# Moving part of GpSimd's elementwise work to VectorE in a fused attention and feed-forward kernel, with a new instruction order

## The chip, the cores and the metric

One NeuronCore of one Trainium2 chip runs the whole program. The metric is device time in microseconds (us) of one execution, as the median of several. TensorE does the matrix products, VectorE and ScalarE the elementwise work, GpSimd some more of it, and SyncE only issues the transfers (DMAs) between memory and the core's on-chip memory. Each engine works through its own list of instructions in order, and semaphores make one engine wait for another.

## What is computed

The reference is attention followed by a normalised feed-forward layer, in float32:

```python
def _attn_ref(q, k, v):                  # (4, 8, 768, 64)
    block, window = 32, 16
    k_sum = k.reshape(B, H, nb, block, D).max(axis=3)
    v_sum = v.reshape(B, H, nb, block, D).mean(axis=3)
    scores_l = where(|i - j| < window, scale * q @ k.T, -1e9)
    scores_s = scale * q @ k_sum.T + log(block)
    a = softmax(concat([scores_l, scores_s]))
    return a @ concat([v, v_sum])

def _moe_ref(x, g_ln, w_ch1, w_ch2):     # x: (4, 768, 512)
    xn = (x - mean(x)) / sqrt(var(x) + 1e-06) * g_ln
    return x + maximum(xn @ w_ch1, 0.0) @ w_ch2
```

Each row sees a window of 31 keys around it and 24 block summaries, and the result of the 8 heads is one row of 512 values, which is normalised, multiplied by a 512 x 2048 and a 2048 x 512 matrix, and added to itself.

## The kernel before, in words

The 3,072 rows are 24 tiles T of 128 rows (`TT`), six to a batch; two tiles are a group g (`NG` = 12) for the feed-forward part. To get the exactness of float32 from 16-bit products, an operand is split into a high part in float16 and a low part, which is what the high part leaves over, and three products of high and low parts are added.

**Stages.** The first batch (T = 0 to 5) is attended in float32 (`attend`, L932), while the weights come in, are merged from their 64-bit form, scaled and split (`fetch_w` to `split_w`, L648 to L755). From T = 6 on, attention goes by split parts (`attend_late`, L942): `load_q`, `load_k`, `load_v` split the inputs; `heads` (L455) makes the scores on TensorE; `late_softmax` (L503) takes the maximum on VectorE, the exponential on ScalarE, the high part of the probabilities on ScalarE and their low part on GpSimd (L521), and sends both through a transposing DMA; `values` (L469) multiplies them with v two tiles later (`LAG`), and `late_out` (L610) divides by the row sums. So the softmax of tile T stands in the list with `values` and `norm` of tile T - 2.

`ln` (L622) normalises a tile: VectorE takes mean and variance; GpSimd adds the constant 1e-6 (L628) and raises to the power -1/2 (L629); VectorE subtracts the mean; ScalarE makes the high part and VectorE the low part of the result (`x16`, L634). `lnT` (L638) sends it through a transposing DMA into `xt`, from which TensorE makes the first product of the feed-forward part (`g1`, L758; tile `h` in the trace). `norm` is the two of them.

For groups 0 to 2 the second product is plain (`g2`). From group 3 on (`PLAIN`) `parts_of` (L785) and `g2_wide` (L827) use a scheme with seven products in place of eight, summed in four PSUM tiles (`acc_a`, `acc_s`, `acc_o`; five for the last group). When the last step of a group (j = 7) is done, the sums are added to the rows: u on ScalarE, v and w on VectorE, and the two additions of u, v and w to the tiles' rows x0 and x1 on GpSimd (L869, L873); the rest on VectorE, and two DMAs store the tiles.

`batch_s` (L371) makes the scales of a batch: VectorE sums, TensorE adds over the partitions (tile `vps`), and VectorE works on that (tile `vm`, L378 and after).

**The order.** The functions only record instructions in a list (`Plan.record`). `Plan.issue` (L158) then issues them in the order of `ORDER`, a packed list of indices worked out beforehand. It sets the place of each instruction on its engine and of each DMA on SyncE; semaphores follow from who reads and writes what. A run of matmuls recorded in a `unit` is one entry. `SOFT` and `WIDE` are 0 before, so that the conditions in L521, L869 and L873 send all of this work to GpSimd.

Every instruction is issued in L163, so the trace tells them apart by their tiles: `p<-p,p` is the low part of the probabilities, `x<-x,uv` the addition to the rows, `rs<-mv` the constant of the normalisation.

Of the kernel before, what the change touches and what calls it, by code (L numbers as in the profile page):

```python
# [24 lines left out]
P = 128  # L25
# [29 lines left out]
SOFT, WIDE = 0, 0  # L55
# [111 lines left out]
def body(ctx: ExitStack, tc, qt, qa, qe, kt, ks, va, vb, vs, g_ln, w1, w2, blocks, out):  # L167
# [335 lines left out]
    def late_softmax(t):  # L503
# [17 lines left out]
        (nc.vector if T < SOFT else nc.gpsimd).tensor_tensor(lo, p, hi, ALU.subtract)  # L521
# [99 lines left out]
    @pl.step  # L621
    def ln(T):  # L622
        x = xt[T]
        s6 = work("s6", f"s6_{T}", [P, 6], F32, 2)
        mv = work("mv", f"mv{T}", [P, 2], F32, 2)
        rs = work("rs", f"rs{T}", [P, 1], F32, 2)
        nc.vector.bn_stats(s6[:], x[:])
        nc.vector.bn_aggr(mv[:], s6[:])  # L628
        nc.gpsimd.tensor_scalar(rs[:], mv[:, 1:2], 1e-6, 0.0, ALU.add, ALU.add)  # L629
        nc.gpsimd.tensor_tensor(rs[:], rs[:], mhalf[:], ALU.pow)  # L630
        xn = stg("xn", [P, DM])
        nc.vector.scalar_tensor_tensor(xn[:], x[:], mv[:, 0:1], gb[:], ALU.subtract, ALU.mult)
# [469 lines left out]
```

## Time and profile before

| | |
|---|---|
| median of 3 runs | 592.65 us (590.61 to 593.58) |
| the profiled execution | 591.7 us, its span 589.9 us |
| TensorE (PE) busy | 577.5 us, 98% |
| VectorE (DVE) busy | 505.0 us, 86% |
| ScalarE (ACT) busy | 437.2 us, 74% |
| GpSimd (POOL) busy | 134.6 us, 23% |
| granted TensorE clock | 1.00 of full speed |

The span runs from the first to the last instruction that the profiler saw; the execution's own time has 1.8 us more around it. Times in the rows are us from the start of the span; a duration is the profiler's, and instructions of one engine overlap a little, so that the start of the next one is often earlier than the end of the last. "PEld" is TensorE's loading of weights, beside its products. "[0.36 <-DVE vm L163]" behind a row means that the engine was idle for 0.36 us before it, and that this wait was ended by VectorE's write of tile vm.

### The profile page before, as it was taken

To read this page: it belongs to the slowest core of one execution; us is meant where nothing else is said; L and a number is where in the kernel's file an instruction comes from. 1 tells how busy PE (TensorE), PEld (TensorE's weight loads), DVE (VectorE), ACT (ScalarE), POOL (GpSimd) and SP (SyncE) were. 2 spreads that over 40 slices of the span, in tenths; PEclk is the share of its full clock that TensorE was granted. 3 is DMA by queue.
4 is the path that set the end of the run, shared out by engine and by line. 5 is a ranking of instruction groups with operands and counts; after the bars stand their busy time and mean duration, and the time that the engine had idled before them with its cause. 6 is when DMAs were issued, how large, how long until landed. Compare 5 with 4: busy or idle time off the path is not lost.

```text
span 589.9 us, 16263 instructions
## 1 busy us (share of the span) xinstructions
PE 577.5 (98%) x6152; PEld 467.0 (79%) x6152; DVE 505.0 (86%) x1326; ACT 437.2 (74%) x1079; POOL 134.6 (23%) x225
## 2 busy tenths in 40 slices
PE   7989999999999999999999999999999999999997
PEld 5557768875555688888889888888788888888886
DVE  4899999999999999899798689898798978676653
ACT  3899998888878789879797665898869476652340
POOL 6142120020114132212414111322311311320101
PEclk9999999999999999999999999999999999999999
DMA  8899899645776568567567363565665522431000
GB/s 298 236 271 306 288 273 259 180 126 143 176 193 170 151 175 172 153 176 169 165 169 165 86 115 100 142 172 139 162 144 138 105 79 64 94 82 37 33 5 37
DMA packets 116260, 90.68 MB, mean 154 GB/s; under 512 B 69597, under 2 KB 100445, under 8 KB 116182
## 3 DMA queue, kind: packets, MB, share of 16 engines
q1 hardware_dynamic: 116182, 89.65, 58.5%
q8 instruction: 48, 0.79, 0.6%
q14 instruction: 30, 0.25, 0.1%
HBM read 67.05 MB, written 6.29 MB: 124 GB/s over the span
## 4 chain that ended last, share of the span: by engine, by line
PE 77%; DVE 8%; DMA 7%; ACT 5%; SPq 2%; issue 1%; ACTq 0%; DVEq 0%
PE h L163 33%; PE acc_a L163 11%; PE a L163 11%; PE acc_s L163 8%; PE acc_o L163 7%; DVE m L163 3%; PE s L163 3%; PE o L163 3%; DMA xt<-x 2%; SPq L163 2%; ACT p L163 2%; DMA qs<-in_qt 1%; DMA qs<-in_ks 1%; DMA raw<-in_w 1%; PE warm L163 1%
## 5 line engine op out<-in xcount | busy, mean ns | idle before, releaser
L163 PE MATMUL h<-xt,w_u 128*128 128x256 f16 x2304 | 263.9, 273 | 1.8 <-DMA xt<-x 1.6
L163 PEld LDWEIGHTS <-w_u 128*128 128x128 f16 x2304 | 224.1, 98 | 32.4 <-issue 2.5
L163 PEld LDWEIGHTS <-h_x 128*128 128x128 f16 x1752 | 169.8, 98 | 46.1 <-DVE h_x L163 0.7
L163 DVE TENSOR_TENSOR h_x<-wide,h_x 128x896 f16<-128x896 f32 x72 | 78.4, 1093 | 17.5 <-ACT h_x L163 16.6
L163 ACT CAST h_x<-wide 128x896 f16<-128x896 f32 x72 | 66.6, 933 | 31.4 <-DVE wide L163 29.9
L163 POOL TENSOR_TENSOR p<-p,p 128x480 f16<-128x480 f32 x36 | 44.8, 1247 | 192.0 <-ACT p L163 153.9
L163 DVE TENSOR_TENSOR wide<-wide 128x128 f32<-128x128 f32 (+1 forms) x224 | 75.4, 345 | 15.1 <-ACT wide L163 12.6
L163 ACT ACTIVATE wide<-h 128x512 f32<-128x512 f32 x72 | 42.5, 590 | 38.4 <-PE h L163 26.7
L163 ACT ACTIVATE p<-p,mn,sv 128x120 f32<-128x120 f32 x144 | 68.6, 477 | 1.3
L163 PE MATMUL acc_o<-w,h_x 128*128 128x256 f16 x408 | 56.0, 273 | 0.0
L163 PE MATMUL a<-w,h_x 128*128 128x512 f16 x240 | 52.6, 379 | 0.0
L163 ACT ACTIVATE bst<-bst 128x384 f32<-128x384 f32 (+2 forms) x55 | 32.3, 588 | 17.2 <-DVE vsum L163 9.7
L163 PE MATMUL acc_a<-mix_x,h_x 128*128 128x256 f16 x324 | 44.9, 273 | 0.0
L163 PE MATMUL acc_s<-mix_x,h_x 128*128 128x256 f16 x324 | 43.9, 273 | 0.0
L163 DVE SCALAR_TENSOR_TENSOR m<-raw,m 128x512 uint32<-128x512 uint32 x64 | 42.6, 685 | 0.1
L163 POOL TENSOR_TENSOR x<-x,uv 128x512 f32<-128x512 f32 x18 | 24.1, 1352 | 80.8 <-DVE uv L163 64.9
L163 POOL TENSOR_SCALAR rs<-mv 128x1 f32<-128x1 f32 x24 | 10.3, 428 | 113.8 <-DVE mv L163 109.4
L163 PE MATMUL acc_a<-w,h_x 128*128 128x256 f16 x216 | 35.8, 273 | 0.2
L163 DVE CUSTOM_DVE_ANT_0 p<-s,mask 128x120 f32<-128x120 f32 x144 | 35.0, 273 | 1.1 <-POOL p L163 1.0
L163 DVE SCALAR_TENSOR_TENSOR kl<-ksg,sv,kh 128x640 f16<-128x640 f32 x36 | 32.2, 895 | 2.2 <-ACT kh L163 1.9
L163 DVE SCALAR_TENSOR_TENSOR v<-vst,sv,v 128x512 f16<-128x512 f32 x36 | 27.9, 775 | 3.8 <-ACT v L163 3.8
L163 ACT ACTIVATE kh<-ksg,sv 128x640 f16<-128x640 f32 x36 | 29.4, 818 | 1.3 <-DMA ksg<-in_kt 1.3
(138 smaller groups left out, 886.7 us busy)
## 6 DMA issues: line engine op xcount, KB each, us to landing
raw<-in_w SPq DMA_DIRECT2D x32, 512.0 KB
ksg<-in_kt SPq DMA_DIRECT2D x36, 368.0 KB
qs<-in_qt SPq DMA_DIRECT2D x72, 128.0 KB
out_x<-x SPq DMA_DIRECT2D x24, 256.0 KB
bst<-in_ks SPq DMA_DIRECT2D x20, 192.0 KB
bst<-in_qa SPq DMA_DIRECT2D x15, 256.0 KB
bst<-in_vs SPq DMA_DIRECT2D x20, 192.0 KB
vst<-in_va SPq DMA_DIRECT2D x36, 96.0 KB
```

Of the source, the lines that this page charges most:

```text
L163: getattr(getattr(nc, engine), op)(*a, **k)
```

## The change

The low parts of the probabilities are taken on VectorE for T >= 18, the last batch (12 instructions); the two row additions of groups 8 to 11 are done on VectorE (8 instructions); the constant of all 24 normalisations is added on VectorE, in place, and GpSimd keeps the power. The rest of GpSimd's work stays. And there is a new `ORDER`.

```diff
-SOFT, WIDE = 0, 0
+SOFT, WIDE = 18, 8
...
@@ late_softmax
         nc.scalar.copy(hi, p)
-        (nc.vector if T < SOFT else nc.gpsimd).tensor_tensor(lo, p, hi, ALU.subtract)
+        (nc.vector if T >= SOFT else nc.gpsimd).tensor_tensor(lo, p, hi, ALU.subtract)
...
@@ ln
         nc.vector.bn_aggr(mv[:], s6[:])
-        nc.gpsimd.tensor_scalar(rs[:], mv[:, 1:2], 1e-6, 0.0, ALU.add, ALU.add)
-        nc.gpsimd.tensor_tensor(rs[:], rs[:], mhalf[:], ALU.pow)
+        nc.vector.tensor_scalar(mv[:, 1:2], mv[:, 1:2], 1e-6, None, ALU.add)
+        nc.gpsimd.tensor_tensor(rs[:], mv[:, 1:2], mhalf[:], ALU.pow)
...
@@ g2_wide
-                (nc.vector if g < WIDE else nc.gpsimd).tensor_tensor(x0[:], x0[:], uv[:, :2].rearrange("p h n -> p (h n)"), ALU.add)
+                (nc.vector if g >= WIDE else nc.gpsimd).tensor_tensor(x0[:], x0[:], uv[:, :2].rearrange("p h n -> p (h n)"), ALU.add)
...
-                (nc.vector if g < WIDE else nc.gpsimd).tensor_tensor(x1h, x1h, twice(w, 0), ALU.add)
+                (nc.vector if g >= WIDE else nc.gpsimd).tensor_tensor(x1h, x1h, twice(w, 0), ALU.add)
```

Unpacked, both values of `ORDER` hold the same 3,111 indices of the same recorded list. Of TensorE's 501 entries 274 stand at another place in its list, none by more than 15 places; of ScalarE's 799 entries 635 are moved, by up to 23 places; of SyncE's 458 DMAs 364, by up to 46; and VectorE's and GpSimd's lists are mixed anew as well. The places that the prediction speaks of:

- TensorE: the last nine entries, the products of steps 1 to 4 of the last group and then its five sums one by one, stand as before. The scores of tile T = 6, half 0 (`s12`, 16 matmuls) now stand ahead of the small product of the second weights' scale (`gram`, `scale_w2`), not behind it. The `vps` product of batch 1 stands behind three more `h` entries. Behind the `vps` product of batch 3 come, as before, 21 and 6 products `acc`, then 16 of `s`; and before the first `h` of group 7 (`h56`) there are now 6 `acc_o` and 3 `acc_a` more, where before there were 3 `acc_a` and 6 `acc_s`.
- VectorE: the low part of `x16` of T = 15 stands right behind the first `vm` instruction of batch 3 that reads `vps`; before, it stood three entries ahead of it. One of the two low parts of the probabilities of T = 18 stands between `late_out` of T = 17 and the low part of its `x16`, the other shortly ahead of the first.
- SyncE: the transposing DMA of `x16` of T = 15 stands right behind that of T = 14.

## Rows read from the trace of the kernel before

**Rows 1.** The page, busy time of each engine over the whole span.
```profile
PE 577.5 (98%) x6152; PEld 467.0 (79%) x6152; DVE 505.0 (86%) x1326; ACT 437.2 (74%) x1079; POOL 134.6 (23%) x225
```
**Rows 2.** Engines by stretch: length; PE, PEld, DVE, ACT, POOL busy; clock, DMA, GB/s.
```profile
0.00:120.00 120.00, 112.59 (x1076) 82.58 (x1076) 107.66 (x327) 102.36 (x323) 31.32 (x112) 1.00 0.91 262
120.00:400.00 280.00, 279.97 (x2992) 220.78 (x2989) 257.70 (x666) 225.45 (x532) 66.49 (x76) 1.00 0.62 153
400.00:560.00 160.00, 158.63 (x1852) 140.22 (x1850) 125.96 (x310) 101.90 (x216) 34.33 (x35) 1.00 0.41 97
560.00:590.00 30.00, 26.35 (x242) 23.37 (x239) 13.68 (x27) 7.46 (x10) 2.49 (x2) 1.00 0.07 26
```
**Rows 3.** The two longest of TensorE's waits: us in total, times, longest.
```profile
PE gain L163 <- DMA xn<-in_g_ln: 3.6, 1, 3.6
PE h L163 <- DMA xt<-x: 1.6, 2, 1.1
```
**Rows 4.** TensorE in order of time, three stalls: start, us, what, idle before.
```profile
104.78 0.38 PE L163 MATMUL vps<-vm,ones 128*128 128x3 f32 x2 [0.36 <-DVE vm L163]
...
119.18 0.35 PE L163 MATMUL gram<-scales,ones 128*128 128x1 f32 x2 [0.54 <-DVE scales L163]
...
419.89 0.28 PE L163 MATMUL h<-xt,w_u 128*128 128x256 f16 x1 [1.11 <-DMA xt<-x]
```
**Rows 5.** Groups by shape: count, busy us, mean ns, idle before.
```profile
L163 POOL TENSOR_TENSOR p<-p,p 128x480 f16<-128x480 f32 x36 | 44.8, 1247 | 192.0 <-ACT p L163 153.9 <-issue 31.9 <-DMA vst<-in_va 5.0
L163 POOL TENSOR_TENSOR x<-x,uv 128x512 f32<-128x512 f32 x18 | 24.1, 1352 | 80.8 <-DVE uv L163 64.9 <-issue 14.7 <-DMA qs<-in_qt 1.2
L163 POOL TENSOR_SCALAR rs<-mv 128x1 f32<-128x1 f32 x24 | 10.3, 428 | 113.8 <-DVE mv L163 109.4 <-DVE rc L163 4.1
...
L163 DVE TENSOR_TENSOR wide<-wide 128x256 f32<-128x256 f32 x80 | 35.2, 440 | 12.8 <-ACT wide L163 12.6
L163 DVE TENSOR_TENSOR h_x<-wide,h_x 128x896 f16<-128x896 f32 x72 | 78.4, 1093 | 17.5 <-ACT h_x L163 16.6
...
L163 DVE TENSOR_SCALAR scales<-scales 128x1 f32<-128x1 f32 x4 | 0.7, 165 | 0.1
```
**Rows 6.** VectorE, GpSimd in order of time, 459 to 463 us, then VectorE at 414.75.
```profile
459.87 1.59 DVE L163 SCALAR_TENSOR_TENSOR v<-vst,sv,v 128x512 f16<-128x512 f32 x1
461.38 1.57 DVE L163 SCALAR_TENSOR_TENSOR qhl<-qs,sv,qhl 64x512 f16<-64x512 f32 x1
...
459.39 3.01 POOL L163 TENSOR_TENSOR p<-p,p 128x480 f16<-128x480 f32 x2 [7.83 <-ACT p L163]
...
414.75 0.73 DVE L163 SCALAR_TENSOR_TENSOR qhl<-qs,sv,qhl 64x512 f16<-64x512 f32 x1
```
**Rows 7.** All engines in order of time, 366 to 373 us: normalisation of T = 15.
```profile
366.79 0.75 DVE L163 SCALAR_TENSOR_TENSOR x<-xn,rs,x 128x512 f16<-128x512 f32 x1 [0.17 <-ACT x L163]
...
367.33 0.28 PE L163 MATMUL vps<-vm,ones 128*128 128x3 f32 x2
...
367.57 1.23 SPq L163 DMA_TRANSPOSE xt<-x  x1
...
368.67 0.16 DVE L163 TENSOR_SCALAR vm<-vps 128x3 f32<-128x3 f32 x1
...
372.05 1.15 PE L163 MATMUL h<-xt,w_u 128*128 128x256 f16 x9
```
**Rows 8.** All engines in order of time, 412 to 416 us: normalisation of T = 17.
```profile
414.08 0.74 DVE L163 SCALAR_TENSOR_TENSOR x<-xn,rs,x 128x512 f16<-128x512 f32 x1
...
415.01 1.27 SPq L163 DMA_TRANSPOSE xt<-x  x1
```
**Rows 9.** All engines in order of time, 582 us to the end.
```profile
582.61 2.49 POOL L163 TENSOR_TENSOR x<-x,uv 128x512 f32<-128x512 f32 x2 [32.74 <-DVE uv L163]
...
585.13 1.14 DVE L163 SCALAR_TENSOR_TENSOR x<-acc_s,scales,x 128x512 f32<-128x512 f32 x2 [0.16 <-POOL x L163]
...
586.39 0.48 DVE L163 SCALAR_TENSOR_TENSOR x<-acc_o,scales,x 128x256 f32<-128x256 f32 x1
```

More of the change, by code (lines that the diff above doesn't have):

```diff
@@ new lines @@
+    "c-lRf30POv7RC3u%pjVxfMXg?DN=!fqKNa5_MCc|BWC7^W2KS4)JiRz9Lw=#YNeS<YNR+Pnv!!4shJaMfaHKE+_T^BQs4XdxYPgKbM{_)?X~y0zE"
+    "VRjYeV@}!{mlKQdu5qvHFO=+~Y2nr;ka1oaX$eR+2w7Q0mGBealR-K2lYJxvnD*^g72;&OCQC{}=TmXMuZDALw1JFW0n@<m)PDw413-rGgyMn#@{"
+    "3%FAzhN2|$U?JQaPj1;Sp$xe57klAC~ny+meIjKeZl$=smo15L%NOSY6-L275Pj+cVDJS7_Kx<1S{!VB(R{o@=vAUjgc80mlrG~T5HP~HM_UM}?*"
+    "Iw5MDa-ZaQd-I|Yc&axT5?u$?aNNOds^FL!5ofn>LM``#_E-s*+*t!Uyv!VAtpv&*FLO0MvklMNsTn?Y=6m7Uz29Ln&$ea?$ZN0TU>d@{wRL(l>D"
+    "yCbbyq0rn-ypGe$N_WxPBs=WT1OFtS9)n0$Lz_h?^pNPFpCy#Nv$HI?5s$ZFfubTZrB+qzJP%T;~V+3!A-dK&I5a+_d7AO2f7d3KGBkcu)`4r*_?"
@@ new lines @@
+    "s9AbUn}{RPa!}&+kY-AOeXZnrltzg$RkgJ7!-^s~WurN+vIC9LBl@HXkY(0;voZI<tkuv|*88TMP1h<?MfORolrfjwT27`L<Ag|&ma^GeET?TJVj"
+    "S$0wz2XHvAPaINwQZv;#pZum)^Qkp40nMRoBQ2drYp&Ztbs!wU%?yt?Oj)R%a}}#v8#hNz=7~Ts7&|2eiwZLcQo#lAk3;Z|G!sMV9JPtuA?HhYgY"
+    "@G6=NSN+apVY(^HE8Q62lbhk&;GHSE7CI&b3X*j!68tYM*@U6sil|y8YN(ApdloWeHn&>g9qTfn_sJ78L(oxq*3-LFP+u!h|8PSio(`Be$F@^RA3"
+    "Dgjoh+hXZ6&CD~2F#}VuB_H~^_1L`B=yCYRm6Reo+p<AWs7XIpM%YOT_(--JG}@qilx52sr{tA>8V9h*Cxt*<1fCf+!a3gsF<BLNowkHc|)feBOO"
+    "Goch{P=YQrLzc}|#)8VfR?n@08zxhb>lhtdqjrh{Y(K0P7nwwkfpT;GwVCemi(udA7MlI}O_b+&y++DcQM#hmFng9yx&v3e8is>&Scqno9R=F1N4"
@@ new lines @@
+    "L9T_sM+0WT>Ic)pWWR(e*<fbdbDC|E>;Z`*_ipPUDMS2TH-p_g;&&Ovs47>qoJ8w={hhl+@G2wcq@mV=`F-_IsiTn`E5p(?^16oW1oNTIm9On3(@"
+    "MHnOI&lLlJ1uP^>yOxHi=}ewQ#hj=4q}(ay0Uj3DI1=CEN5x?Vw+oZMwv&{$w0U;G89&OAie)=gH15>_Is$$u`*}%068T8w0TAK5F16`O?y6NdlU"
+    "a#To~}JdX8$mW48xV;GDor!Sd)($P*eDf*3kr048za{@NCMSmLbA0W-(LU~p`p)K_h3R4~(-7jK_wWZw;)_#(SIv9;7e)~*0^z@R(=>c<CN7=omr"
+    "Tx(O!s`V4F}XOx{$v6``4jULxOqrqnoC+2Yd@2rwz^!wp5tH|1HU8msKlYf*ELRR%TCS-sM%$(NU~AbF%~V{F6YobA1zBxT#;;e?JJMLo?7Oz4K}"
+    "G}vAtktIg?#Klc-5fA_^6vqf9$(!Khq)$F$NGnqV^ZO=*Mu;U-0<!tH1>Wj>ydl*zWbsmrQIG{;UipJK1*GbSFzg(J4Axo5{X2W(TBX8+@SW*^wG"
@@ new lines @@
+    "PNpr=soG6L`ORY4CiHQ!`e*?wN0|#+Pohwy6f;LBl2OO?C0SudP+9t!uXF^;wZIKB$=F?FM`Bl^d}MtMA=9yDuRbdaY?L`}hd4{!Qs%C$D=oO{XF"
+    "`aD4{>-TJKW#Zl_4fj=h;`B#dfrOqK)N*bzu5fb61wRsxLdc-HGx6dOg@#=GH|Q&yn*D%`X}RAFk*;e!Fb%%d6&)`$#U>0eI#w$>eXYrrBENqOB<"
+    "xWQcq$&**tuM~=vF^QD__M#1M@deQcER=Oii8nd0#zu@8{eNswmtXT+q#>-;c*DTd!=FZ~jOOAs+?9@c_fwscGnUYFgC)m*@S?|f$;Pb8|!lG2FS"
+    "b?O-QFj-<4Kuz}-PZO+JngHG$egiy#KxPA+DU$ZKY_Yb`pH_Nc856n!^RlXRCdcQfIQ23k)UycN>tWlpp0wL!IR7}R2J!as?$*3{}jbpZ;RwD#>d"
+    "**@`fZ!eUB;D1!sfuWZDodlm_OgeP8|Mb#!E>9S3jbqP$1sE9%%Dn`B(NjR8b{zKqfgZ7GG4g({YkS*&%8%J{05HDP*{y7-$NNe-o(2rz4-E?FBd"
@@ new lines @@
+    "FUfFFSg9j*mmOltNq2oiK9M!lzsITKMYg}0pdZOhJnn2?B#WQ759CK_M2-YVU+Qps{QsGpIIIDtg>7e6lhModHkz~?eX608bqZWhr%pInRAi@_X>"
+    "<d=jNJ}?P4MD~{#&l=J<dK-AB?ubhq01|in{tM9ac5o>>{s`nNd`g-jbnhWID4Z$Rsi`ihOCsxW(k}(<oeTEyJ@=GZ3|nw~wSZReXl&Kz)ps9w<p"
+    "W`4_9Ll@(-VZ8MCXWiT54ELQC$V~w<gC)0Ec*b;pWGpop<Y<&_f_(8tZ)#T<&@GX_GX);IG!nZB*FRbb#-nGLyoag@~7Rk~8Y^fX4UO(U}Q@+uw^"
+    "jk}`Kv(M!nLy{b4i>$vy<`RY@s6{)I6yWt&zIuTwN<A|Jx5hbla?}pxhKMy&rwtq9V9;n)id-`KJuA<t`RVQ6dJr(0*S<nXlxj@=aF@>p$<N+qMn"
+    "wf<7y=H=w))~T6;O`+={XazC@#Y3G|eu=!4#tDO9Z#dbkaYzo(O=f_4M9qi9Mu=d8PfUTvy#$~~Y#wxRQzhSI_0;Pn&o9Pj)@r#Mska||UTf2Vdu"
@@ new lines @@
+    "QoVc1R-NEXbGPC7M(s-f_7&NBka*0apWUHLbewb7Jq$7f<!yN0%4u)cF{d9mhtTzg5iiyM=ydw$t=gQbyMuMl>J@VNy7r}?2$4ec`*|JjGzPc#VP"
+    "F?3Q?c3U)<wJ9O0kJ1D??fH4D*+VukBz*S2)@W`>4wL1l;;UuVHVv)52cH%fT|2N)~Jf$pX{Zp4W#a!sh<-^o;uy-P0lcOXIO{EtR1iJR4_D^ZZ3"
+    "wZU)%znel5nqbbCHkZjP`(a6p4wmKcmeULtejsDb~T_{lwn)kil#^b#*QdiQ0-Z7up7_7Yv51Wzqzpz3PGdlEnW#tZ5z$CN4o~BzGBLlRi6Ke0#Y"
+    "qcoppZZBJ`sX6z*a^*wm2N0ZFIh*2d>`~<$>r;0zo(cNz_kgHs!jKMQn!<12Vn9AcowHGupjt<Uu(ktsq7-IGs4r^j^Z&RUNSY4J;r<N9VYS4DEh"
+    "K2dq}^b<FMLUH<(T+-VCe=WRH`<vm^S3PJkCP*dwKY_!M&rA3xL|^*ghOsNF=XHkpZbzs@A`fz-$}`jS#)WT>16iCFOZg`PB;t|Ce5n?p7h{SL>o"
@@ new lines @@
+    "GwhYJHHeur;HfW_Wwm}l5Br*?nPrx`fQ_Y4niEv17eLTRZ!_N}u*Pw{Mc=U*E%*WbiDsRK5@D9|TUYwQDPR=IT?>>ToX&M1$XGIR82-;BXV#N(7s"
+    "$U_*m#vVmo+QwEQyfsv`{N?eOTUOSM;Nn*F1TKomwLKlt|<^YIXCn&e94d4$G&ptMj3==uD<kpNP*%9i$6nJDFLHU05pDMLLdk+hg%VP+F`j=)nd"
+    "u(@3uN<4<MzOTB)1x(q@KOUd`_E?bv8$)InphwrEK5?qU*4&20s-LQ|kg@(S3BGjiIw*|du&<jN^wo6;)*g!YmnjWq-xsZgF3G8IH@LnU<^7gZh#"
+    "N+dQ{Q~7!2DjIv$v$}5nf=ssY;wTeMd|j?Q{N`vme6x{z|$>g^+dXmI$*a18|ShQXoFf-Gq>r&hcfyB>O6>={3gn=0u}8^4HzuTO8l9DwkCsavYv"
+    ";1bLCy#N;i9wJ}-}+v4bpUcj95amD-oV&ds1p-)la5yD0ka((rtsjN|$MNWVbUvt<7k?GCOt)niw6va5@vu~Iv-=oR>JSU+Z5D*gs>pQB%sQycXR"
@@ new lines @@
+    "+C3LUJCavjs7U+hQx?g1-9UaH#WwHV;b`}V@Z^1}`eAn2W6APAu%SPd`WBj1l}fS*=I+84?+e0CvNH{}C}h@6=u}7gj3F>TjlF*v80Jr$XQFrh+~"
+    "3tjAk!L7&*B_MT?~Y!Az)WP{VRnomX|!TaTvDUhN+%1tOk?O(u;Er+OSD`&~yG-vO``(c6EluJ&2;$8@;9DsETWd^f0vGGyN4MyQV3iIUgJH;N(K"
+    "~5nIUm+4!`XJ;F!)HjF55gOUB!-^|tFJZXdXOHg|Q-gl^d8(3pFd$BaEe4hOL6imM$_pazRdOd%bp3Kan=w$;~zmSou@Sr~`I|w|Js1M=jLNGfyg"
+    "=-$hX>fNHSoX!%S|~$LvN0RKi}9{DHv7?w_{$gYsS6%AlSCL3Lo5sRD>${BUakgc<*{Ba4A>3&rND6~Xy#z`QX&*71=N<l<od^0^fn6kiN1y%J9Q"
+    "J9v4v{u^}RR9h<YevhK)8+WJH9tqRND#p25T}h`JqyjYoAmF+M~t??7q7!Mz(DOmEm#9)46n-x|QXEzA{1#%_YA<*=rYj%6><5dQAQf_5mNr^{8a"
@@ new lines @@
+    "`WTtB4V}ngkKUCCKf&Dou%H<uqR8vBDD9{E3hM+*3|Z*qUlx9b%G0PvKHl#|le@#IuAp2Ijt#|*Yjh<8$?R+@@--|v!#SI3{tkFVvv2B549>&ZD4"
+    "urX`Yp61UcO~iG`3$S|Bj>k<Io4o3JbwBOHYx#UQb&S{$%4r7pnPzl5bRvsSQ=Y!jF+pqZ)tVMO&^blPS3+)pNZ5Kn9+pB5eh~eyls5y>|vX<m0G"
+    ")chn@FdeoW<dzb1MhGu#d)~g9A=+<OVSOo_8x<&_}s!yX%36jcj5?t7iO1y`a+tHEKlKRq=jv<5IxEQq^iMn2eFIjNm-^4!&FYAKjx1jbdV}GI3I"
+    "tTWV(wHtlQS;I;;VNV5!Lda!@-F?|`=It6{#QV~#xOdDnNL&mW6<@-Wi)vZK!u8diQf0Qm1InNIyNH{;n*BWRIk>i!kB}^*r#L%q2SP-(P#0i2T?"
+    "r_U$ar-^_=%$WfEfwm?0R1dcwv?@#@?y>hx|D&B3cUdixyx6olq+?e$TWz;6P5;|+G~(@MS=<x^8r$k%!tPwNBJIuSn|vd;mFv5arQe37g^Nd8+A"
@@ new lines @@
+    "<p;!NB214Yvl@fNIBz~iyh1G<k6$;5bSQb)5EgVo)qmAI`s%AC>QoiR<#Rl%vx!=PzRI|4ogoYGHI^JQMB@@#^D2Cem9jE|+BF?N+o0XA5sL_UoW"
+    "Gj%jH_Yb8C?KcxAAzOjwE8<cdmwTpbi-ofW>#z`vzJEORwr#cz6u<-@?*%Xoz<=f_n3axI}_pe{kFcM~>4Uc93+kw;0Xxav~5Ee<bQ**fT{}mh4O"
+    "n6)H-+z07ztYy_EhgI&UC=B-H07)}IBfo(5Vzsk`;&5MXbGdhH2SUR7)@*yLhVuldZuRD5Hk*p3zv6_I5<@hZ6=n#oG)^1y}T04&MbQj(ig^~DPP"
+    "@?_@-MK}ta+iOvb0|YL`=Abgf%y%sfeQCwSGW)REAabvcDvq})jU+NJDQh{-?vbTd+_!?c@~5Pp3ViA#Nr{l_*>w7g=e|^|Gl2ajVe4}MfMj`Sq6"
+    "gKLiUq4$V;z!d;McJ*ZFYdH>~jH3_<||c(YK;5ie6R<}vEnBkEQy&gP#{2J6d7aLJSV*i^_U7o88mR?kWUlKwn-2$S#NX8{;h#WrtU^N;n9l^p+`"
```

53 lines of the change are left out of this document (1 added, 52 removed).

## The prediction

> **What bounds the kernel now.** I read the busy times of the page first: TensorE is busy for 577.5 of 589.9 us, VectorE for 505.0, ScalarE for 437.2 and GpSimd for 134.6 [rows 1]. So TensorE has 12.4 us of idle time, and nothing can save more than that unless it takes products away, which this change doesn't.
>
> The table by stretches tells where those 12.4 us lie [rows 2]. In the first 120 us TensorE is idle for 120 - 112.59 = 7.4 us; from 120 to 400 for 0.03 us; from 400 to 560 for 1.4 us; in the last 30 us, of which the span has 29.9, for 3.6 us. The list of TensorE's waits names the largest [rows 3]: 3.6 us at the very start, until the first vector of data lands, and 1.6 us in two waits of the first feed-forward product for the transposed rows `xt`. In order of time [rows 4], 1.11 us of that is one stall at 419.89, and in the first 120 us the single waits are of the size of 0.36 us (104.78, for `vm`) and 0.54 us (119.18, for the scale of the second weights). The granted clock is 1.00, the upper level, in every stretch [rows 2], so no clock is there to be won.
>
> At the end the last product starts its sums at 586.39 and the store follows [rows 9]: 589.9 - 586.39 = 3.5 us that no engine's list can shorten. What an order can win is therefore 12.4 - 3.6 - 3.6 = 5.2 us: 3.8 in the first 120 us and 1.4 around 420 us. The profiled execution took 591.7 us, span 589.9 and 1.8 around it. The sum below is made against 591.7, which lies 0.95 us under the median of 592.65 and within the runs shown.
>
> **The change part by part.** *The work itself.* GpSimd loses 12 low parts at 1.247 us, 8 row additions at 1.352 us and 24 constants at 0.428 us: 15.0 + 10.8 + 10.3 = 36 us [rows 5]. For VectorE no row shows the 128x480 subtraction. Two neighbours of the same kind stand on either side of it: 440 ns for 256 columns and 1,093 ns for 896, so 653 / 640 = 1.02 ns a column [rows 5]; 480 columns come to 440 + 224 x 1.02 = 668 ns and the 512 of a row addition to 701 ns. The ends are the neighbours themselves, 0.44 and 1.09 us. The constant is one element per partition, 165 ns in the nearest row [rows 5]. VectorE gets 12 x 0.668 + 8 x 0.701 + 24 x 0.165 = 8.0 + 5.6 + 4.0 = 17.6 us.
>
> Of this, the 12 low parts, 6 additions (the last two come after 582 us) and 8 constants fall between about 400 and 560 us: 8.0 + 4.2 + 1.3 = 13.5 us. VectorE is busy there for 125.96 of 160 us [rows 2], and would be for 139.5, 87%. From 120 to 400 us it is busy for 257.70 of 280, 92%, and TensorE loses 0.03 us in that stretch. So by load alone the added work costs nothing: its cover is TensorE's own 158.6 us of work in that stretch. If VectorE's idle time there were gone, 13.5 us would have to fit in nowhere and would show; it isn't, by 20 us.
>
> GpSimd's loss is worth nothing directly: it is not on TensorE's path. Its last two additions, 582.61 to 585.10, end before the last product's sum at 586.39, and what waits for them, 0.16 us on VectorE, does so while TensorE still works on the last bank [rows 9]. The last nine entries of TensorE are unchanged. End: 0; the bounds are 0 and, if the two additions hold VectorE up behind the last product, 1 x 0.70.
>
> *The new order, first 120 us.* The scores `s12` now fill the wait of 0.54 us ahead of the weights' scale [rows 4]: -0.5. The `vps` product moves back behind three `h` entries, so its wait of 0.36 us goes, but the `h` entry behind it comes no earlier than its buffer is read, so I take 0 there. The other waits are ended by VectorE, ScalarE and DMAs in about equal parts, and VectorE gets six constants of 0.165 us, 1.0 us, in the same stretch, where it is busy for 107.66 of 120 us [rows 2]. I take -0.5 for the stretch; the bounds are -3.8 (every wait after the start gone) and +1.0 (the six constants passed on whole). DMAs in this stretch are busy at a share of 0.91 [rows 2] and 364 of 458 are moved over the program; what that does to a landing no row tells, and it is in these bounds.
>
> *The new order, `h56`.* Before, the low part of `x16` of T = 15 (366.79, 0.75 us) ran ahead of `vps` (367.33), its DMA was issued at 367.57, and `h56` began at 372.05 without a wait [rows 7]. Now it stands behind a `vm` instruction that reads `vps`. From the start of `vps` that makes 0.28 + 0.16 + 0.75 us and then the DMA, at most the 372.05 - 367.57 = 4.48 us of before: 5.67 us. TensorE has as many products between `vps` and `h56` as before, 372.05 - 367.33 = 4.72 us. The wait is 5.67 - 4.72 = 0.95 us if the landing took all of the 4.48, and 0 if it took 3.5. Behind it on VectorE the split of `h55` waits, which the next sums need. I take +0.9, as this is the same DMA.
>
> *The new order, `h64`.* This is the stall of 1.11 us: the low part at 414.08, DMA at 415.01, landed for 419.89 [rows 4, 8]. Now one low part of the probabilities and one constant, 0.67 + 0.17 us, stand between the row division and this low part on VectorE, and a second low part shortly ahead. The bounds are 0 (VectorE had idle time there) and 2 x 0.67 + 0.17 = 1.5; I take +0.5. At the other first products of a group, the nearest rows give 0 (`h56`, as it was) to 1.1 (`h64`): I take 0 and keep +1.3, two low parts, as the end.
>
> Sum: 0 - 0.5 + 0.9 + 0.5 = +0.9, 591.7 + 0.9 = **592.6 us**, the median of before within its noise.
>
> **One rule weighed against the rows.** While GpSimd takes two low parts, 459.39 to 462.40, VectorE's splits of v and q take 1.59 and 1.57 us; without them the split of q takes 0.73 [rows 6]. So each such overlap costs VectorE 0.8 us, and the change ends those of the last batch. The Trainium skill, GPSIMD Engine Reference, section "8. Key points", states that GpSimd shares its SBUF interfaces with VectorE and contends with VectorE instructions that have two SBUF inputs. The trace agrees with 1.57 against 0.73 us. By that rule the change would give back part of the 13.5 us and could come out faster, which is the first rival; my sum has none of it, as VectorE isn't the bound.
>
> **The rivals.** *Faster.* The contention ends, the normalisation loses a GpSimd instruction of 0.428 us [rows 5] and gains one of 0.165, and the order has the products arrive when their data does. Then the 1.4 us around 420 and half of the 3.8 us go: 591.7 - 3.3 = 588.4. For it: one such stall is 1.11 us by itself, and low parts of 1.25 us become 0.67. Against it: the first 120 us have no low part and no addition that moves.
>
> *Slower: late transposes.* The place is VectorE's list ahead of each first product of a group; the price is two low parts, 1.34 us, at two of the four groups that begin after 400 us, the 0.95 us of `h56`, and the 1.0 us of six constants early: 591.7 + 2.7 + 0.95 + 1.0 = 596.3. It decides from the point at which the DMA is issued less than about 4.5 us before TensorE reaches the product [rows 7, 8]; both rows stand right at that point, which speaks for it. Against it: VectorE has 20 us left in that stretch.
>
> *VectorE as the bound* from 400 to 560 us would need over 20 us more than I count; less than 1 in 50, left inside the slower case. That the change doesn't do what it says I rule out: with both constants at 0 all of this work is on GpSimd before, and the turned conditions send just the last batch and the last four groups to VectorE.
>
> **How the numbers follow.** A measurement of this kernel tells about 0.5%, 3.0 us, from no change. The forecast and its own bounds near it (590 to 595) have 0.72; faster than 589.7 takes three of the 5.2 us, 0.13; slower than 595.6 takes the late transposes at several groups at once, 0.15. The range goes from 589.4, half of the early waits gone (592.6 minus 3.2), to 596.4, which takes in the slower case and the upper ends of `h56`, `h64` and the early constants.
>
> **What would show it.** Right: TensorE's busy time stays near 577.5 us; VectorE's rises by 12 to 18 us, with low parts of about 0.67 us; GpSimd's falls to about 100; `h <- xt` leads the waits again with 2 to 3 us, among them one at the first product of group 7; the wait at the scale of the second weights is gone; splits of v and q stay at 0.75 us after 400. Wrong: TensorE's idle time outside start and end falls below 3 us (faster), or three or more groups begin with a stall of over 1 us (slower), or a stretch after 400 us shows TensorE waiting for splits on VectorE, which would make VectorE the bound.

## The result, and the profile after

The changed kernel takes 598.79 us (median of 6 runs, 596.92 to 602.62), the kernel before 591.67 us (6 runs, 590.61 to 593.58): a ratio of 1.0107, 95% interval 1.0072 to 1.0142. That is slower by 1.1%, with an interval clear of 1, and outside the predicted range, above its upper end of 596.4. Timed a second time the changed kernel has 598.15 us and the ratio 1.0100 (1.0075 to 1.0124).

The profiled execution has a span of 597.6 us, 7.7 us over that of before. The page, busy times of each engine:

```profile
PE 580.6 (97%) x6152; PEld 468.2 (78%) x6152; DVE 514.1 (86%) x1370; ACT 440.1 (74%) x1079; POOL 101.4 (17%) x181
```

TensorE's idle time is 597.6 - 580.6 = 17.0 us against 12.4 [rows 1], and the products themselves take 3.1 us more. The table by stretches of the changed kernel (columns as in [rows 2]) says where:

```profile
0.00:120.00 120.00, 110.68 (x1022) 79.71 (x1023) 103.46 (x319) 97.85 (x310) 32.22 (x107) 0.99 0.90 259
120.00:400.00 280.00, 279.96 (x2999) 220.51 (x2998) 258.67 (x684) 228.00 (x535) 59.13 (x64) 1.00 0.60 150
400.00:560.00 160.00, 156.16 (x1828) 137.97 (x1827) 132.76 (x333) 102.64 (x221) 10.01 (x10) 1.00 0.47 105
```

Idle: 9.3 us in the first 120 us against 7.4 [rows 2], none from 120 to 400 as before, 3.8 us from 400 to 560 against 1.4. The granted clock of the first stretch is 0.99, no longer 1.00. TensorE's waits, where [rows 3] stood before, and the four longest behind the start in order of time:

```profile
PE gain L162 <- POOL spare_x L162: 3.6, 1, 3.6
PE h L162 <- DMA xt<-x: 2.8, 2, 1.8
PE h L162 <- DVE m L162: 2.0, 1, 2.0
PE acc_a L162 <- DVE h_x L162: 1.6, 1, 1.6
```
```profile
89.25 2.78 PE L162 MATMUL h<-xt,w_u 128*128 128x256 f16 x24 [1.01 <-DMA xt<-x]
...
114.42 7.83 PE L162 MATMUL h<-xt,w_u 128*128 128x256 f16 x55 [2.05 <-DVE m L162]
...
419.21 0.28 PE L162 MATMUL acc_a<-w,h_x 128*128 128x256 f16 x1 [1.58 <-DVE h_x L162]
...
426.87 0.39 PE L162 MATMUL h<-xt,w_u 128*128 128x256 f16 x2 [1.81 <-DMA xt<-x]
```

They are the first product of group 1 (89.25), the first product of group 2 (`h16`, 114.42), the sums of group 7 that wait for a split on VectorE (419.21), and the first product of group 8 (426.87, `h64` of the prediction). Before, the first had 0.46 us, the last 1.11 us [rows 4], and the other two none. The wait of 0.54 us ahead of the weights' scale [rows 4] is gone.

Behind the one of group 2 the clock fell to the lower of its two levels, 1.2 GHz, for 3.4 us; the table by stretches of TensorE alone (busy, clock, DMA share, GB/s):

```profile
114.00:115.40 1.40, 0.98 (x9) 1.00 0.76 228
115.40:118.80 3.40, 3.40 (x19) 0.50 0.28 80
118.80:120.00 1.20, 1.20 (x12) 0.99 0.12 26
```

3.4 us at half speed cost 1.7 us. Of the six runs three have a mean granted clock of 0.996 or 0.997 and take 599.4 to 602.6 us; the three with 1.000 take 596.9 to 598.2.

The moved work itself, groups by shape (columns as in [rows 5]):

```profile
L162 POOL TENSOR_TENSOR p<-p,p 128x480 f16<-128x480 f32 x24 | 28.1, 1172 | 111.6 <-ACT p L162 68.8 <-issue 31.5 <-DMA vst<-vsum 10.5
...
L162 DVE TENSOR_TENSOR p<-p,p 128x480 f16<-128x480 f32 x12 | 7.7, 649 | 2.0 <-ACT p L162 2.0
L162 DVE TENSOR_TENSOR x<-x,uv 128x512 f32<-128x512 f32 x8 | 5.5, 688 | 0.2
L162 DVE TENSOR_SCALAR mv<-mv 128x1 f32<-128x1 f32 x24 | 3.5, 145 | 0.2
```

It adds 7.7 + 5.5 + 3.5 = 16.7 us to VectorE, whose busy time rises by only 9.1 us.

### The profile page after: what moved, and what is told of

It reads as the page before. It is cut to its first block, busy times and chain, and to the rows that moved or that the text cites. A ratio compares the mean times of both kernels' runs of the same rounds, so it can differ in the third digit from the quotient of the medians.

```text
span 597.6 us, 16255 instructions
## 1 busy us (share of the span) xinstructions
PE 580.6 (97%) x6152; PEld 468.2 (78%) x6152; DVE 514.1 (86%) x1370; ACT 440.1 (74%) x1079; POOL 101.4 (17%) x181
## 4 chain that ended last, share of the span: by engine, by line
PE 74%; DVE 12%; DMA 8%; SPq 2%; ACT 1%; issue 1%; ACTq 0%; DVEq 0%
PE h L162 32%; PE acc_a L162 11%; PE a L162 10%; PE acc_s L162 7%; PE acc_o L162 6%; DVE m L162 4%; PE s L162 3%; PE o L162 2%; DMA raw<-in_w 2%; SPq L162 2%; DMA vst<-in_va 1%; DMA ksg<-in_kt 1%; DVE h_x L162 1%; DMA spare_x<-in_va 1%; DVE p L162 1%
## 5 line engine op out<-in xcount | busy, mean ns | idle before, releaser
L162 DVE TENSOR_TENSOR wide<-wide 128x128 f32<-128x128 f32 (+1 forms) x224 | 74.0, 340 | 13.5 <-ACT wide L162 11.4
L162 POOL TENSOR_TENSOR rs<-mv,mhalf 128x1 f32<-128x1 f32 x24 | 21.7, 905 | 211.3 <-DVE mv L162 199.1
L162 POOL TENSOR_TENSOR p<-p,p 128x480 f16<-128x480 f32 x24 | 28.1, 1172 | 111.6 <-ACT p L162 68.8
L162 ACT ACTIVATE qhl<-qs,sv 128x512 f16<-128x512 f32 x36 | 25.7, 713 | 6.4 <-DMA qs<-in_qt 4.2
```

Source lines behind the costliest of these rows:

```text
L162: getattr(getattr(nc, engine), op)(*a, **k)
```

## The experiments

**Which part of the change.** Two theories stood against each other: the new order, or VectorE's added work. Two kernels take the parts alone, two take half the order.

e1_engines is the kernel before with the new conditions and constants of the change, whose core is

```diff
-SOFT, WIDE = 0, 0
+SOFT, WIDE = 18, 8
...
-        nc.gpsimd.tensor_scalar(rs[:], mv[:, 1:2], 1e-6, 0.0, ALU.add, ALU.add)
+        nc.vector.tensor_scalar(mv[:, 1:2], mv[:, 1:2], 1e-6, None, ALU.add)
```

and e2_order is the kernel before with the other list:

```diff
-order = old
+order = new
```

> The new placement of the low parts, additions and constants on VectorE, in the old order. If the new order is the cause: the time of the kernel before within 0.3%, 590 to 593.5 us, GpSimd busy for about 100 us, no stall of over 1.2 us after the start. If VectorE's added work is the cause: 596 to 599 us, with waits for VectorE after 400 us.

> The new order with all three kinds of work left on GpSimd. If the new order is the cause: 596 to 600 us, with the stalls of about 2 us near 114 us and of 1.5 to 2 us near 420 us still there. If VectorE's added work is the cause: 590 to 593.5 us.

Measured: e1_engines 592.29 us, ratio 1.0002 (0.9989 to 1.0015); e2_order 600.15 us, ratio 1.0132 (1.0115 to 1.0149). The order is the cause, and the placement alone costs nothing. Stalls of the placement alone, and below it of the order alone:

```profile
411.83 0.28 PE L161 MATMUL acc_a<-w,h_x 128*128 128x256 f16 x1 [0.95 <-DVE h_x L161]
419.14 5.41 PE L161 MATMUL h<-xt,w_u 128*128 128x256 f16 x48 [1.16 <-DMA xt<-x]
```
```profile
114.09 8.02 PE L161 MATMUL h<-xt,w_u 128*128 128x256 f16 x72 [2.23 <-DVE h_x L161]
...
417.79 0.28 PE L161 MATMUL acc_a<-w,h_x 128*128 128x256 f16 x1 [1.37 <-DVE h_x L161]
424.59 5.41 PE L161 MATMUL h<-xt,w_u 128*128 128x256 f16 x48 [1.02 <-DMA xt<-x]
```

The stall of over 2 us at group 2 is there with the order alone. The placement has one of its own, 0.95 us at the sums of group 7, and still ends where the kernel before does.

e3_early and e4_late have the placement, and the new order for the first or for the last part of the list:

```diff
-order = new
+order = new[:1271] + [i for i in old if i not in new[:1271]]
```
```diff
-order = new
+order = old[:1271] + [i for i in new if i not in old[:1271]]
```

> The new placement; the new order for the first 1271 of 3111 entries (up to about 201 us), the old one behind. By the trace of after, the early part lost 4.9 of the 7.7 us of span: 595.5 to 597.5 us if the order is the cause and its two parts add up. 594 to 595 us if the late loss is VectorE's work, which this kernel has too, and the early one is half chance.

> The new placement; the old order for the first 1271 entries, the new one behind. By the trace of after the late part lost 2.7 us: 593.5 to 595.5 us if the order is the cause and the parts add up, with the stalls near 420 us and without the one near 114 us; equal to the run of the placement alone if the late stalls come from VectorE's work.

Measured: 595.63 us, 1.0053 (1.0033 to 1.0073), and 593.52 us, 1.0020 (1.0003 to 1.0036). The early half loses more, the late half less than the trace of after had it; its interval overlaps that of the placement alone (0.9989 to 1.0015), so a loss by the late half is not shown. Together 0.73%, against 1.07% for the whole: within the intervals, or the two help each other; that stays open.

g3_no_soft has the placement without the low parts, in the old order:

```diff
-SOFT, WIDE = 18, 8
+SOFT, WIDE = 24, 8
```

> The new placement in the old order, but with all low parts left on GpSimd: additions and constants alone move. If the low parts on VectorE are what made the split for group 7 late (a stall of 0.95 us there with them, 0.09 without): that stall is under 0.3 us, and the time 0.3 to 1 us less, ratio 0.9975 to 0.9995. If VectorE's added work costs nothing: the ratio of the run with them, 1.000 within 0.15%.

Measured: 592.46 us, 0.9997 (0.9977 to 1.0018). The stall at the sums of group 7 is gone, as expected of the low parts; the time isn't, for the trace has others instead:

```profile
112.27 5.40 PE L161 MATMUL h<-xt,w_u 128*128 128x256 f16 x48 [0.92 <-DMA xt<-x]
...
420.99 5.41 PE L161 MATMUL h<-xt,w_u 128*128 128x256 f16 x48 [0.80 <-DMA xt<-x]
```

**What makes group 2 late.** The page names VectorE's tile `m` (the merging of the weights) as what ended the wait at 114.42 and `h_x` (the split of the feed-forward values) in e2_order, but `h16` reads neither: the last that it needs is the transposing DMA of T = 5, as the row of g3_no_soft says. SyncE's issues of it, after and before:

```profile
107.09 0.33 SPq L162 DMA_DIRECT2D raw<-in_w  x1
107.75 1.29 SPq L162 DMA_TRANSPOSE xt<-x  x1
```
```profile
104.67 0.33 SPq L163 DMA_DIRECT2D raw<-in_w  x1
106.01 1.25 SPq L163 DMA_TRANSPOSE xt<-x  x1
```

TensorE was ready for `h16` at 114.42 - 2.05 = 112.37, 4.6 us after the issue; before, it began at 110.62, 4.6 us after the issue too. So it was issued no later beside the product that needs it. It landed later. Its semaphore takes sixteen steps: before, all between 110.07 and 110.22; after, fifteen from 112.80 to 112.95 and the sixteenth at 114.33. Two things differ. The 512 KB load in front (`raw`) was issued 0.66 us ahead, not 1.34; and during the transpose the DMA's instruction queue moved one packet of 16 KB (before, there was one of 8 KB on another such queue, 14). The packets by queue in its flight, 107.75 to 114.4 us after and 106.01 to 110.6 before:

```profile
q1 hardware_dynamic: 1734, 1.56, 108.9%
q8 instruction: 1, 0.02, 1.1%
```
```profile
q1 hardware_dynamic: 1433, 1.08, 112.1%
q14 instruction: 1, 0.01, 0.4%
```

The page counts 48 packets on queue 8 in the whole run; 6,152 products and 6,152 weight loads by 48 are 256 TensorE instructions for each. I took this for the fetch of TensorE's instructions, one in 256. f1_raw takes the load away, f4_late the loads ahead of two DMAs in the late part, and two kernels move the fetch. f1_raw, SyncE's list in the trace's names:

```diff
-raw<-in_w
 xt<-x
+raw<-in_w
 qs<-in_qt
```

> The changed kernel with one entry of SyncE's list moved: the 512 KB load of the last raw weight block but one behind the transpose of T = 5 instead of right ahead of it. If that load in front of the transpose makes the first product of group 2 late: its stall of 2.05 us falls under 0.3 us, and 2 us of lower clock behind it (in about half the runs) with it: 594.5 to 597 us, ratio to the kernel before 1.004 to 1.008. If the stall is only the instruction fetch of 16 KB that falls into the transpose: it stays if the transpose still ends after 112.1 us, and is gone if it ends before. If neither: stall and time as in the changed kernel, about 1.0107.

Measured: 597.41 us, 1.0072 (1.0048 to 1.0097). The first fifteen steps came 2.8 us after the issue, not 5.2, and the first product of group 2 doesn't wait. The time is not told apart from the changed kernel's (1.0072 to 1.0142): VectorE waits for the load instead, and TensorE for the split behind it:

```profile
114.98 0.43 DVE L161 TENSOR_SCALAR m<-raw 128x512 uint32<-128x512 uint32 x1 [2.27 <-DMA raw<-in_w]
...
117.14 2.13 PE L161 MATMUL h<-xt,w_u 128*128 128x256 f16 x18 [1.57 <-DVE h_x L161]
```

f4_late:

```diff
-vst<-vsum
 ksg<-in_kt
 qs<-in_qt
+vst<-vsum
...
-ksg<-in_kt
 xt<-x
+ksg<-in_kt
```

> The changed kernel with two entries of SyncE's list moved: a 12 KB load of the sums behind the K load of step 39 instead of ahead of it, and the K load of step 41 behind the transpose of T = 17 instead of ahead of it. If the queue in front of these two is the cause of the stalls of 1.58 us (sums of group 7) and 1.81 us (first product of group 8): both fall under 0.8 us, 1 to 2 us less than the changed kernel, ratio 1.007 to 1.009. If the instruction fetch holds the transpose up: the stall of group 8 stays between 1 and 2 us, and the time is that of the changed kernel within 0.2%.

Measured: 597.24 us, 1.0084 (1.0055 to 1.0112), not told apart from the changed kernel. Both stalls fell, to 0.37 and 0.25 us, though the sixteenth step of the transpose of T = 17 came 1.68 us behind the fifteenth and a 16 KB packet lay in its flight; the fifteenth came 2.7 us after the issue, not 5.8. And the scores of a later half now wait for the load that was put back:

```profile
421.41 5.41 PE L161 MATMUL h<-xt,w_u 128*128 128x256 f16 x48 [0.25 <-DMA xt<-x]
428.91 0.24 PE L161 MATMUL s<-kh,qhl 128*64 128x120 f16 x2 [1.20 <-DVE qhl L161]
```

**Moving the fetch.** f5_phase (changed kernel) and f6_before_phase (kernel before) put more instructions in front:

```diff
-for i in range(WARM):
-    nc.tensor.transpose(ps[:, i % 4 * P : i % 4 * P + P], ident[:], ident[:])
+for i in range(2 * WARM):
+    nc.tensor.matmul(ps[:, i % 8 * 64 : i % 8 * 64 + 64], ident[:], ident[:, :64], start=True, stop=True)
```

> The changed kernel with the 36 warm-up transposes of 128 columns written as 72 products of 64 columns: the same columns, 72 instructions more on TensorE, so that each later 16 KB fetch of its instructions, one in 256 instructions, comes about 4 us earlier beside the other work. If the fetch is what makes the transposes of T = 5 and T = 17 land late: the stall at the first product of group 2 falls from 2.05 to under 0.6 us, the one of group 8 from 1.81 to under 0.5 us, 3 to 5 us less unless other transposes are hit instead: ratio 1.002 to 1.007. If the queue of loads is the cause: stalls and time as in the changed kernel, 1.009 to 1.013.

> The kernel before with the same 72 narrow warm-up products. If the fetch is the cause, its stall of 1.11 us at the first product of group 8 goes (its fetch came at 417.49 us, in the transpose): 0.5 to 1.5 us less, unless a fetch now falls into another transpose; ratio 0.997 to 1.001. If it isn't: the stall stays and the ratio is 1.000.

Measured: 621.18 us, 1.0492 (1.0462 to 1.0522), and 617.44 us, 1.0411 (1.0387 to 1.0435). Both miss what was expected, by a cost I hadn't counted: each of these float32 products is two instructions of 215 ns, so the warm-up took 31.0 us, not 6:

```profile
5.51 30.98 PE L163 MATMUL warm<-ident 128*128 128x64 f32 x144
```

The times say nothing on the fetch. g1_phase (changed kernel) and g2_engines_phase (placement, old order) do it with transposes:

```diff
-for i in range(WARM):
-    nc.tensor.transpose(ps[:, i % 4 * P : i % 4 * P + P], ident[:], ident[:])
+for i in range(2 * WARM):
+    nc.tensor.transpose(ps[:, i % 8 * 64 : i % 8 * 64 + 64], ident[:64], ident[:64, :64])
```

> The changed kernel with the 36 warm-up transposes of 128 columns written as 72 of 64 columns (one instruction each, about half as long): TensorE's list is 72 instructions longer in front, so each later instruction fetch comes some 4 us earlier beside the other work, near 108 and 420 us in place of 112.09 and 424.10. If the fetch is what makes the last step of the transposes late: the stall of group 2 falls from 2.05 to 0.6 us or less, that of group 8 from 1.81 to 0.5 or less; 2 to 4 us less unless another transpose is hit: ratio 1.003 to 1.008. If the queue of loads alone does it: stalls as they were, ratio 1.009 to 1.013.

> The new placement in the old order, with the same 72 short warm-up transposes. Its fetch at 416.59 us, in the transpose of T = 17, would come near 412.7, ahead of it. If the fetch is the cause of the 1.16 us at the first product of group 8: that stall is under 0.4 us, 0.5 to 1.5 us less than without, ratio 0.996 to 0.999. If not: the stall stays, ratio 1.000.

Measured: 601.06 us, 1.0138 (1.0103 to 1.0174), and 598.05 us, 1.0079 (1.0048 to 1.0109). The totals are missed. The warm-up takes 7.9 us, and the scores behind it take 1.13 us for sixteen products where they took 0.67; from about 20 us on they take 0.67 again. The stalls of group 8 went as the fetch theory has it, from 1.81 to 0.30 us (g1_phase) and from 1.16 to none (g2_engines_phase); but the unchanged kernel has none there either in its second trace (k1_again, below), so these two runs don't settle it. At group 2 the stall fell from 2.05 to 1.28, not to the 0.6 expected, for the late landing of all sixteen steps, 5.4 us after the issue, is left:

```profile
116.70 5.51 PE L162 MATMUL h<-xt,w_u 128*128 128x256 f16 x49 [1.28 <-DVE m L162]
...
428.86 3.34 PE L162 MATMUL h<-xt,w_u 128*128 128x256 f16 x29 [0.30 <-DMA xt<-x]
```

Over 14 traces (before, after, and all runs but f5_phase, f6_before_phase and the four below with one engine's list), with 24 transposes of `xt` each, 336 in all, 24 have a sixteenth step 1.38 to 1.68 us behind the fifteenth. In all 24 a 16 KB packet began 0.56 to 0.86 us ahead of the fifteenth step. Of the other 312 transposes only 12 had one within 1.1 us, two of them in that same range (T = 5 of g3_no_soft and k1_again) and not late. Before the change the stall of 1.11 us at group 8 was this as well: fifteen steps by 418.23, the sixteenth at 419.85, the packet at 417.49.

**Mending the places.** f7_both is f1_raw with VectorE's three instructions that wait for the load (`m`) put behind the split (`h_x`) that TensorE waits for:

```diff
-m<-raw
 vm<-vm
-m<-raw
 sv<-vm
-m<-raw,m
 h_x<-h,h_x
...
+m<-raw
+m<-raw
+m<-raw,m
```

> The changed kernel with two places moved: SyncE's 512 KB load behind the transpose of T = 5, as in the run before, and VectorE's three instructions that wait for that load behind the split of the last sums of group 1. If the wait was only handed on from the transpose to the split, as the run before showed (1.57 us): no stall over 0.5 us between 100 and 125 us, and no low clock behind it: 594 to 596.5 us, ratio 1.002 to 1.006. If something else holds group 2 up: a stall of over 1 us there again, ratio 1.007 or more.

Measured: 598.80 us, 1.0102 (1.0066 to 1.0139). Group 2 begins on time, and 0.3 to 1.1 us are lost at each of five places from 118 to 212 us, the first of them

```profile
118.30 2.78 PE L161 MATMUL h<-xt,w_u 128*128 128x256 f16 x24 [1.10 <-DVE h_x L161]
```

k1_again is the changed kernel once more; k2_mended has the moves of f1_raw and f4_late together.

> The changed kernel itself, timed and profiled again. Ratio 1.009 to 1.013. If the fetch of TensorE's instructions sits at the same place in the program each time: stalls of 1.5 to 2.3 us at the first product of group 2 and of 1 to 2 us at that of group 8 again, with a fetch in both transposes. If they were chance of one run: one of the two is under 0.6 us.

> The changed kernel with the three transfers moved on SyncE's list as in the two runs with single places (the 512 KB load behind the transpose of T = 5, the 12 KB load behind the K load of step 39, the K load of step 41 behind the transpose of T = 17). If the loss is the waits for these transfers: ratio 1.002 to 1.006, with no stall of over 1.3 us. If such waits are only handed on to the next: 1.006 to 1.010, with stalls of about 1.2 to 1.6 us at splits and scores that wait for the loads that were put back.

Measured: 598.15 us, 1.0100 (1.0075 to 1.0124), and 596.33 us, 1.0076 (1.0060 to 1.0092). The second profile of the same kernel has other stalls: 0.88 us at group 2, where the packet came at 112.45 and the sixteenth step wasn't late, 2.01 at the sums of group 7, none at group 8, and a low clock behind the 2.01:

```profile
418.96 0.28 PE L162 MATMUL acc_a<-w,h_x 128*128 128x256 f16 x1 [2.01 <-DVE h_x L162]
```
```profile
419.50:422.80 3.30, 3.30 (x20) 0.50 0.83 209
```

So a single stall is partly chance, and the sum isn't. k2_mended has 1.69 and 1.40 us at the split and the scores that wait for the loads put back, as the handing-on theory has it, but all its six runs have a mean clock of 0.999 or more and lie within 596.0 and 597.2 us. That is 0.3% less than k1_again beside it, with intervals that overlap, so a gain by the moves is not shown:

```profile
115.27 5.69 PE L161 MATMUL h<-xt,w_u 128*128 128x256 f16 x48 [1.69 <-DVE h_x L161]
...
430.14 0.24 PE L161 MATMUL s<-kh,qhl 128*64 128x120 f16 x2 [1.40 <-DVE qhl L161]
```

**One engine's list at a time.** Four kernels have the placement and the new order on some engines alone, with the entries left out of it that the other lists forbid. The diff is that of the list:

```diff
-order = old
+order = merge(new on SyncE, old elsewhere)
```

> The new placement; SyncE's list in the new order (but for 2 of 458 entries that the other lists forbid), all other lists in the old one. If the moved transfers carry the loss: ratio 1.006 to 1.011, with stalls of 1 us or more at first products of a group. If they don't: 1.000 to 1.002.

> The new placement; the lists of VectorE and ScalarE in the new order (but for 13 entries), the others in the old one. If the order of the work on these two carries the loss: ratio 1.006 to 1.011. If the transfers or TensorE's list do: 1.000 to 1.003.

> The new placement; TensorE's list in the new order (but for 2 of 501 entries), the others in the old one. If TensorE's list carries the loss: 1.006 to 1.011. If products that are merely moved by a few places cost nothing by themselves: 1.000 to 1.004, as a product that is moved ahead of what feeds it waits.

> The new placement; the lists of VectorE, ScalarE and TensorE in the new order (but for 7 entries), SyncE's in the old one. If the transfers carry the loss: 1.000 to 1.004. If the lists of the engines do: 1.007 to 1.012, that of the whole change.

Measured: 1.0946 (1.0915 to 1.0977), 1.1440 (1.1405 to 1.1474), 1.0741 (1.0702 to 1.0780) and 1.0886 (1.0853 to 1.0919): every expectation missed by far. The longest waits of h1_sp and h2_va:

```profile
507.62 0.61 PE L161 MATMUL acc_a<-w,h_x 128*128 128x256 f16 x2 [6.07 <-ACT h_x L161]
```
```profile
594.53 1.87 PE L160 MATMUL h<-xt,w_u 128*128 128x256 f16 x8 [7.42 <-DVE x L160]
```

With one list out of step the engines wait for each other up to 7.4 us at a time. The loss of 1% can't be laid on one engine's list this way; the question which list carries it stays open, and may have no answer.

No version beat both kernels: the placement alone, with or without the low parts, equals the kernel before within its interval.

## Why the prediction was wrong

- **What bounds the kernel** held: TensorE, idle only in the first 120 us and near 420 us. "No clock is there to be won" was true and left out that it can be lost: 1.7 us in this profile.
- **The work itself** held: 649, 688 and 145 ns against 668, 701 and 165 taken, GpSimd at 101.4 us, and by load no cost (e1_engines 1.0002). VectorE rose by 9.1 us, under the 12 to 18 named. The rule of the Trainium skill, GPSIMD Engine Reference, section "8. Key points", that GpSimd contends with VectorE instructions that have two SBUF inputs, agrees in direction: from 400 to 560 us the split of q takes 735 ns on the mean, 822 before. As argued, none of it reached TensorE.
- **The first 120 us** is the step that failed. It had -0.5, with +1.0 as its upper bound, and put 364 moved DMAs "in these bounds" without a price. All that TensorE does from 130 us on is about 4.8 us late in the trace. 2.6 us of it had come together by the first product of group 1 (89.25 us, 86.68 before): 1.0 us of waits and 1.6 us in early products that took longer, 1.0 of it in the float32 scores, for which no run shows the reason. The other 2.2 us came at group 2: its stall of 2.05 and 1.7 for the clock, less 0.9 us of waits that are gone (0.36 and 0.54 [rows 4]) and 0.6 in small pieces. The stall is a transpose that landed 6.6 us after its issue where 4.2 were taken before and 4.6 were there. Over ten runs the early half of the order costs 0.53%, 3.1 us (e3_early); which landing or which list carries it stays open. The same row of a landing, 4.9 us at `h64` [rows 4, 8], stood in the prediction and was used only for the groups after 360 us.
- **`h56`** was wrong: +0.9 taken, no wait measured. The prediction read the 4.48 us from issue to product as the landing; by its semaphore the DMA landed 2.7 us after its issue before (367.57 to 370.29) and 2.8 us after (373.35 to 376.12), 0.8 us ahead of `h56` at 376.90.
- **`h64`** was right in size, +0.7 (1.81 against 1.11) for +0.5, and wrong in cause. I put it on VectorE's list; TensorE was ready 4.0 us after the issue, 3.8 before, so the list didn't make it later; the transpose was held up in flight, 5.8 us where 4.8 were taken before. k1_again has no stall there at all.
- **The sums of group 7** weren't in the sum: 1.58 us. The low parts on VectorE alone make 0.95 at that place (e1_engines, and none of it in g3_no_soft), the order alone 1.37 (e2_order); in the changed kernel the chain is SyncE's K load, 5.1 us from issue to use where it took 4.1 before, then ScalarE, VectorE and the split. With that load one place earlier 0.37 is left (f4_late):

```profile
407.09 0.45 SPq L162 DMA_DIRECT2D ksg<-in_kt  x1
...
412.19 0.83 ACT L162 ACTIVATE kh<-ksg,sv 128x640 f16<-128x640 f32 x1 [2.18 <-DMA ksg<-in_kt]
413.05 0.89 DVE L162 SCALAR_TENSOR_TENSOR kl<-ksg,sv,kh 128x640 f16<-128x640 f32 x1 [2.38 <-ACT kh L162]
```

- **The end** held: 597.6 - 593.82 = 3.8 us from the last product's sums, 3.5 before.
- **The signs.** Two of the three signs of being wrong came: three groups begin with a stall of over 1 us (1.01, 2.05, 1.81), and after 400 us TensorE waits for a split on VectorE (1.58). VectorE isn't the bound for that, being idle for 27 of 160 us there. The low end of the range, 589.4, is said to be half of the early waits; that half is 1.9 us, and 3.2 were taken.
- **The rivals.** "Late transposes" is what happened, at 596.3 us too low and with a chance of 0.15 too small. Its point of decision, less than about 4.5 us from issue to product, would not have told: at group 2 that distance is 4.6 us in both traces, and what changed is the landing, 4.2 to 6.6 us. Its place was wrong, DMAs in flight rather than VectorE's list, and it had no clock. "Faster" fell: the contention did end, and it was worth nothing.

## What to carry to other kernels

Where TensorE is 98% busy, a new order has little to win and every landing to lose: list each DMA that TensorE waits for with its spare time between landing and use, and price a reordering by those that have under 1 us of it (here 0.4 us at group 2), DMAs in front of them included. Time the parts of such a change apart before reading stalls: the placement was free and the order was not, and a stall that is mended is mostly handed to the next. An order worked out over all engines is one piece; one list of it alone is worth nothing.

## What the runs showed of the hardware that was not expected

- A 16 KB packet on the DMA's instruction queue comes once in 256 TensorE instructions (48 a run, 49 with the 216 more of f5_phase), at places that moved with the count of instructions in front. Where it began 0.56 to 0.86 us ahead of a transpose's fifteenth completion, the sixteenth was 1.4 to 1.7 us late in 24 of 26 cases, and never without one. Where it began 2.3 to 2.7 us ahead, at the transpose of T = 17 in four traces, the fifteenth step came 4.5 to 5.8 us after the issue; in nine others 2.7 to 3.6 (in three of them the K load stands behind it or further ahead), in one 4.4. The Trainium skill, DMA: Bandwidth & Descriptors, section "Why a DMA increments its semaphore by 16 and not by 1", says that a DMA runs on up to 16 engines that finish independently, and its section "Queues, rings and completion order" that the increment lands only after every earlier write of its DMA engine, across that engine's queues. The trace agrees with the first, a sixteenth step 1.4 to 1.7 us behind fifteen others; by the second a packet on that one engine could hold the step up, and that it does is argued from the times, not shown.
- Behind stalls of 2.05 and 2.01 us TensorE was granted half its clock for 3.4 us; behind two of 2.23 and 2.19 us (e2_order, f4_late) it was not, nor, in the same 14 traces, behind any of 1.81 us or less.
- A 512 KB load issued 0.66 to 1.34 us ahead of the transpose of T = 5 made it slower by 1 to 2.7 us: fifteen steps 3.8 to 5.5 us after the issue in eleven traces with it, 2.7 to 2.8 in the three without (f1_raw, f7_both, k2_mended).
- Behind warm-up transposes of 64 rows, 7.9 us long (g1_phase, g2_engines_phase), sixteen score products took 1.13 us; behind those of 128 rows, and from about 20 us on, they take 0.67. The profile's clock column says 1.00 throughout, so it doesn't show what slowed them.
